# A Mamba2 scan that feeds a four-branch feed-forward merge: the spreads of two chunks, the weight sums' places and the last step's order are changed

## The chip, the cores and the metric

The kernel runs on one core of one Trainium2 chip. The time is the device time of one execution in microseconds (us); the profile is of one such execution. Engines: TensorE (PE, its weight loads PEld), VectorE (DVE), ScalarE (ACT), GpSimd (POOL) and SyncE (SP), which here only issues DMAs. PSUM banks hold 512 fp32 per partition.

## What is computed

All is fp32. First a state-space attention per batch (4), head (8) and 768 positions, with head size 32 and state size 16; `la = log(clip(a))`:

```python
L = exp(cum[i] - cum[j]) * causal          # decays inside a chunk
y = (C @ B.T * L) @ x + (C @ state) * exp(cum)
state = exp(sum(la)) * state + sum_j(B_j x_j * exp(cum[-1] - cum_j))
```

Its output, 3072 tokens of 256 channels, is the input of four feed-forward branches (256 to 1024 to 256), merged by normalised probabilities `p`:

```python
h = maximum(x @ w1[e], 0)
out += p[:, e:e+1] * (h @ w2[e])
```

The kernel works with chunks of 128 positions, since the result doesn't depend on the chunk length.

## The kernel before

**Tiling.** There are 24 chunks of 128 tokens; four of them, one from each batch, make a block of 512 tokens, and six blocks make the run. For each block the feed-forward part takes 8 steps (four branches, two halves of the hidden size), 48 in all, numbered n; r is the step's number in its block.

**Attention of a chunk** (chunks 0 to 3 stand ahead of the loop, L694 to L770). `spread` multiplies the chunk's decays by ones, so that each partition has all of them in PSUM; a_q holds them on one partition in 32, and four row tiles of 32 partitions (L322) do four quarters of 256 columns each. `decays` runs VectorE scans over them (L355) and gives the lower triangle LT; GpSimd multiplies its last column with B (L360). `masks` (ScalarE, L369) prepares C from the chunk's tokens `xb`, `scores` multiplies it with B (L384) into four quarters g, `masked` (VectorE, L396) multiplies g by LT. For chunks 0 and 1 one quarter goes `aside`: ScalarE copies it (L403) and GpSimd multiplies (L404). `outputs` multiplies by the tokens (L430), and ScalarE copies the result to yT and A (L439 to L446). From chunk 3 on the decays come spread from DRAM (`load_decays`, L125), where `store_decays` has put them.

**The gate.** `turn_gates` transposes the probabilities (L288), ScalarE copies them (p_sb, L291), SyncE stores them (L292), `spread_gate` (L300) spreads those of block 0. The bank of that spread comes from a ring of two (tag "att") that the y of the chunks use as well.

**Feed-forward by seven products.** Each pair of 2x2 block products is done with seven products in place of eight (from step 2 on): `fmul` (L491) the first ones, with `snap` (ScalarE), `total`, `gated` and `diff` (VectorE) between, and `smul` (L576) the second ones, one step later. They need four sums of weight blocks. In the first block `sum_w1` and `sum_w2` make them on GpSimd, four adds and one store each (L180 to L198); later blocks load them. GpSimd works in program order, and a step's sums wait for nothing but their weights.

**The order is written out by hand.** Every engine takes its instructions in program order; the loop L774 to L868 writes one step. A step's VectorE order is: total 11, gated 11, then the work left from the step before (two `diff`, L520, and a `carry` of a state, L454 to L461), the first half of a chunk's scan if the step has one (r of 0, 2, 4, 5), `total` 22 (L503), which TensorE's next products into bank Y (L491) wait for, and so on.

**The end.** `finish` does the last step's second products in the order 1, 3, 6, 7, 5, 2, 4, adds them to the four quarters of o (channels by tokens; d is the half of the channels, b1 and b2 the halves of the tokens), turns each back by TensorE (L627), copies it to SBUF and stores whole rows: one store of 256 KB and two of 128 KB. Blocks ahead of the last are turned by VectorE in blocks of 32 (`turned_out`, L665) and leave by `leave`: eight stores of 16 KB for each chunk, in pieces of 32 numbers, on SyncE's queue (L673).

Of the kernel before, what the change touches and what calls it, by code (L numbers as in the profile page):

```python
# [12 lines left out]
P = 128  # L13
# [4 lines left out]
def kernel(  # L18
# [255 lines left out]
    nc.gpsimd.tensor_copy(a_cut, a_sb)  # L274
    nc.gpsimd.memset(a_cut[:, :, 0:1], 0.0)

    def store_decays(kind):
        d, sb = ((acut_d, a_cut), (ac_d, a_sb))[kind]
        nc.scalar.dma_start(
            out=d.rearrange("c h s -> (c h) s").rearrange("(p r) s -> p r s", r=2), in_=sb)  # L280

    gate = {}

# [27 lines left out]

    yT, yS = {}, {}

    def spread(c, homes):


        s = st[c]
        s["a"] = []
        for q, (pool, tag) in enumerate(homes):
            k = slice(32 * q, 32 * q + 32)  # L320
            b = pool.tile([P, NT * P], FP32, tag=tag, name="a")
            nc.tensor.matmul(  # L322
                out=b, lhsT=ones[k], rhs=a_q[k, c].rearrange("p t s -> p (t s)"),
                start=True, stop=True, tile_position=(32 * q, 0))
            s["a"].append(b)

    def decays(c):
        for part in range(3):
            decay_part(c, part)
# [60 lines left out]
    def masked(cs, rs):  # L390
        for r in rs:
            for c in cs:
# [1 line left out]
                h = slice(NT * q, NT * q + NT)  # L394
                s = st[c]
                nc.vector.tensor_mul(s["MT"][:, h, 0:P], s["g"][q], s["LT"][:, h])  # L396

    def aside(c, q):

        s = st[c]  # L400
        h = slice(NT * q, NT * q + NT)
        g = att.tile([P, NT, P], FP32, tag="gs", name="gs")
        nc.scalar.copy(out=g, in_=s["g"][q])  # L403
        nc.gpsimd.tensor_mul(s["MT"][:, h, 0:P], g, s["LT"][:, h])  # L404

    state = {}

# [201 lines left out]
    def finish(n):  # L609


        k = n // SPB
        add = nc.vector.tensor_add
        b1, b2 = slice(0, HB), slice(HB, BLK)
        o = ffn.tile([P, 2, BLK], FP32, tag="o", name="o", bufs=1)
        u = ffn.tile([P, 3, HB], FP32, tag="u", name="u", bufs=1)
        turned, rows = {}, {}

        def turn_out(b, d):
            if b not in turned:  # L620
                rows[b] = ffn.tile([P, 2, DM], FP32, tag="z", name="rows", bufs=3)
                turned[b] = [ps_f.tile([P, DM], FP32, tag=tag, name="turned") for tag in "XY"] \
                    if b == 0 else ps_att.tile([P, 2, DM], FP32, tag="att", name="turned")
            for i in range(2):
                lo = b * HB + i * P
                t = turned[b][i] if b == 0 else turned[b][:, i]
                nc.tensor.transpose(t[:, d * P:d * P + P], o[:, d, lo:lo + P], ident[:, 0])  # L627

        def dst(b):
            return out.rearrange("(i k p) m -> k p i m", k=NBLK, p=P)[k][:, 2 * b:2 * b + 2]  # L630

        smul(n, 1)
        smul(n, 3)
        keep(k, 0)
        p1, p3 = kept[k, 0][:, 0], kept[k, 0][:, 1]
        smul(n, 6)
        add(u[:, 0], acc[k, 2][:, 0], p1)
        add(u[:, 1], u[:, 0], p3)
        smul(n, 7)
        smul(n, 5)  # L640
        p7, p5 = acc[k, 1][:, 0], acc[k, 1][:, 1]
        add(u[:, 2], p7, u[:, 0])
        add(o[:, 1, b2], p5, u[:, 2])
        add(o[:, 0, b2], p5, u[:, 1])
        smul(n, 2)
        add(o[:, 0, b1], acc[k, 2][:, 1], p1)
        turn_out(1, 1)
        smul(n, 4)
        turn_out(1, 0)
        nc.scalar.copy(out=rows[1], in_=turned[1])  # L650
        nc.sync.dma_start(out=dst(1), in_=rows[1])
        turn_out(0, 0)
        add(o[:, 1, b1], acc[k, 3][:, 0], u[:, 2])
        turn_out(0, 1)
        nc.vector.tensor_copy(rows[0][:, 0], turned[0][0])
        nc.sync.dma_start(out=dst(0)[:, 0], in_=rows[0][:, 0])
        nc.scalar.copy(out=rows[0][:, 1], in_=turned[0][1])
        nc.scalar.dma_start(out=dst(0)[:, 1], in_=rows[0][:, 1])

    def turned_out(k):  # L660

# [2 lines left out]
        ot = kept[k, "ot"] = ffn.tile([P, 2, BLK // 32, 32], FP32, tag="ot", name="ot", bufs=1)  # L664
        nc.vector.transpose(ot.rearrange("p d b j -> p d (b j)"), o)  # L665

    def leave(k, c):

        dst = out.rearrange(
            "(c k b i) (d a j) -> c k a d i b j", k=NBLK, i=32, b=P // 32, j=32, d=2)[c, k]  # L670
        for q in range(P // 32):
            for d in range(2):
                nc.sync.dma_start(  # L673
                    out=dst[q, d],
                    in_=kept[k, "ot"][32 * q:32 * q + 32, d, P // 32 * c:P // 32 * (c + 1)])

    def opened(n):

# [3 lines left out]


    homes = ((ps_s, "acc0"), (ps_s, "acc1"), (ps_att, "att"), (ps_att, "att"))
    banks = ((ps_f, "X"), (ps_f, "Y"), (ps_s, "acc2"), (ps_s, "acc3"))

    def turn(n, w=4):

# [4 lines left out]

    turn(1)  # L694
    turn(1, 2)
    spread(0, banks)
    turn(1, 3)
    masks(0)
    scores([0], homes)
    decays(0)  # L700
    masks(1)
    spread(1, banks)
    aside(0, 3)
    masked([0], (2, 0, 1))
    store_decays(0)
    turn_gates(ps_att, "att")
    store_decays(1)
    outputs([0])
    scores([1], ((ps_s, "acc0"), (ps_s, "acc1"), (ps_att, "att"), (ps_f, "X")))
    decays(1)  # L710
    aside(1, 3)
    spread_gate(ps_att, "att")
    masked([1], (0, 1, 2))
    spread(2, ((ps_s, "acc2"), (ps_s, "acc3"), (ps_f, "Y"), (ps_s, "acc0")))
    masks(2)
    outputs([1])
    sum_w1(0, 0)
    load_decays(3)
    load_w2(1)
# [54 lines left out]
    for n in range(PLAIN, NS):  # L774
        k, r = divmod(n, SPB)

        ahead = CPB * (k + 1)
        scanned = [ahead + d for d in {0: [0], 2: [1], 4: [2], 5: [3]}.get(r, [])]
        scored = [ahead + d for d in {3: [0, 1], 6: [2, 3]}.get(r, [])]
        done = [ahead + d for d in {4: [0, 1], 7: [2, 3]}.get(r, [])]  # L780
        if k == NBLK - 1:
            scanned, scored, done = [], [], []
        ending = r == 0 and k > 0
        e = r // JJ
        if r % JJ == 0 and n + JJ < NS:
            load_gate(*divmod(n // JJ + 1, E))
        if PLAIN + 2 < n + 2 < NS:
            load_w1(n + 2)
            load_w2(n + 2)
        opened(n)  # L790
        total(n, 1, "11")
        gated(n, "11", "z11")
        for work in late:
            work()
        if r == 1 and k > 0:
            combine(k - 1, 0)
            combine(k - 1, 1)
        for c in scanned:
            decay_part(c, 0)
        for c in scored:  # L800
            masks(c)
        if k > 0 and 2 <= r < CPB + 2:
            leave(k - 1, r - 2)
        smul(n - 1, 1)
        fmul(n, 6)
        snap(n, 6)
        smul(n - 1, 3)
        if ending:
            keep(k - 1, 0)
        if done:  # L810
            outputs(done)
            states.extend(done)
        fmul(n, 5)
        fmul(n, 7)
        snap(n, 7)
        total(n, 7, "22")
        smul(n - 1, 7)
        smul(n - 1, 5)
        if ending:
            keep(k - 1, 1)  # L820
        gated(n, "22", "z22")
        if r == 1 and k > 0:
            combine(k - 1, 2)
        for c in scanned:
            decay_part(c, 1)
        for c in scored:
            decay_part(c, 2)
        if n == PLAIN:
            sum_w2(0, 1)
        elif n == SPB - 4:  # L830
            sum_w1(n + 2)
        elif n >= SPB - 3:
            sum_w2(n)
        if n < CPB:
            load_chunk(n + CPB)
        for c in scanned if n >= CPB else []:
            if c + 2 < NCH:
                load_decays(c + 2)
        for c in done:
            if c + CPB < NCH:  # L840
                load_tokens(c + CPB)
                load_heads(c + CPB)
        fmul(n, 3)
        total(n, 6, "12")
        fmul(n, 4)
        gated(n, "21", "X")
        gated(n, "12", "z12")
        if r == SPB - 1 and k < NBLK - 1:
            sums(k + 1)
        smul(n - 1, 6)  # L850
        if scored:
            scores(scored, ((ps_att, "att"), (ps_att, "att"), (ps_f, "Y"), (ps_f, "X")))
            masked(scored, (3, 2, 0, 1))
        smul(n - 1, 2)
        diff(n, "T3", "22", "12")
        smul(n - 1, 4)
        if n == PLAIN:
            sum_w2(1, 1)
        if n != SPB - 4:
            sum_w1(n + 2)  # L860
        if PLAIN < n < SPB - 4:
            sum_w2(n + 1)
        diff(n, "T1", "12", "11")
        if r == 1 and k > 0:
            turned_out(k - 1)
        late = [lambda n=n: diff(n, "T2", "22", "T1"), lambda n=n: diff(n, "T4", "21", "T2")]
        if states:
            late.append(lambda c=states.pop(0): carry(c))  # L868
# [48 lines left out]
```

## Time and profile before

| | |
|---|---|
| median of 3 runs | 639.71 us (639.64 to 640.04) |
| profiled execution | 639.64 us, of which the span is 637.9 |
| busy: TensorE, VectorE, ScalarE, GpSimd | 632.2, 483.7, 119.1, 109.7 us |
| first feed-forward product (L540) starts | 13.29 us |
| steps 5 and 6 of the loop | 78.02 to 90.10, 90.10 to 103.87 us |
| last block's first product in `finish` | 626.40 us |
| last store issued, last byte moved | 634.55, 636.5 us |

A line of the timeline gives the start, the time, the engine (a q behind its name: its queue, for DMAs and waits), the line of the code, the operation, out<-in by the program's names, the shape, and how many instructions were merged into the line (consecutive ones of the same kind; each fp32 product counts as two). In square brackets is the idle time ahead of it and what ended it. A line of the waits gives the waiter, what it waited for, and the total, the number and the longest in us. For a DMA the time is that of its issue; the transfer comes later.

### The profile page before, as it was taken

The page shows a single profiled execution, that of the slowest core. Times are in us where ns is not written, and L with a number is a line of the kernel's source. Part 1 is how long each engine was busy: PE and PEld are TensorE (multiplying, and loading weights), DVE is VectorE, ACT ScalarE, POOL GpSimd, SP SyncE. Part 2 cuts the span into 40 slices and gives each one's busy share as a digit, 9 for nine tenths or more (in the row PEclk, how much of TensorE's full clock was granted, in tenths as well). Part 3 has the DMA queues.
Part 4 walks back from the last instruction along what each step waited for, and adds up shares of the span by engine and source line. Part 5 has one row for each costly group of instructions (what it writes and reads, how often), then busy time and mean ns, then how long its engine had stood idle before and what let it go on. Part 6 is the DMA issues. An engine that isn't in the chain of part 4 may idle for free.

```text
span 637.9 us, 9231 instructions
## 1 busy us (share of the span) xinstructions
PE 632.2 (99%) x3407; PEld 537.1 (84%) x3407; DVE 483.7 (76%) x811; ACT 119.1 (19%) x259; POOL 109.7 (17%) x159
## 2 busy tenths in 40 slices
PE   9999999999999999999999999999999999999997
PEld 5888887888888888888888888888888888888886
DVE  7869998887787688777687778768877667756555
ACT  4011221212111221122211211212121211111110
POOL 6788556020000002000002000001100000100000
PEclk9999999999999999999999999999999999999999
DMA  7987893855766392666284567639364834266000
GB/s 231 320 317 271 288 340 136 288 178 167 189 200 237 94 364 73 230 190 242 92 293 142 172 202 189 230 121 341 97 207 152 275 136 133 63 181 210 1 1 33
DMA packets 97248, 121.61 MB, mean 191 GB/s; under 512 B 28840, under 2 KB 80436, under 8 KB 97204
## 3 DMA queue, kind: packets, MB, share of 16 engines
q1 hardware_dynamic: 94376, 111.20, 53.6%
q0 software_dynamic: 2304, 9.44, 3.8%
q8 instruction: 27, 0.44, 0.3%
q10 hardware_dynamic: 524, 0.39, 0.2%
q14 instruction: 17, 0.14, 0.1%
HBM read 108.16 MB, written 12.83 MB: 190 GB/s over the span
## 4 chain that ended last, share of the span: by engine, by line
PE 98%; DVE 1%; ACT 0%; issue 0%; DVEq 0%
PE acc L576 43%; PE X L491 25%; PE Y L491 19%; PE acc L557 2%; PE y L430 2%; PE g L384 2%; PE X L540 1%; PE Y L540 1%; PE y L418 1%; PE t L691 1%; PE a L322 0%; DVE hT L520 0%; DVE h L513 0%; DVE z L503 0%; PE gp L300 0%; PE turned L627 0%
## 5 line engine op out<-in xcount | busy, mean ns | idle before, releaser
L503 DVE TENSOR_TENSOR z<-Y,snap 128x512 f32<-128x512 f32 x138 | 94.6, 685 | 123.5 <-ACT snap L498 72.7
L576 PE MATMUL acc<-hT,wt 128*128 128x256 f32 x736 | 181.2, 379 | 0.0
L498 ACT COPY snap<-X 128x512 f32<-128x512 f32 x138 | 80.8, 586 | 464.6 <-PE X L491 388.1
L576 PEld LDWEIGHTS acc<-hT,wt 128*128 128x128 f32 x736 | 139.8, 190 | 19.0
L576 PE MATMUL acc<-h,wt 128*128 128x256 f32 x552 | 142.5, 381 | 0.0
L491 PE MATMUL X<-yS,wt 128*128 128x256 f32 x552 | 141.7, 379 | 0.0
L576 PEld LDWEIGHTS acc<-h,wt 128*128 128x128 f32 x552 | 104.1, 190 | 17.1 <-issue 3.0
L491 PEld LDWEIGHTS X<-yS,wt 128*128 128x128 f32 x552 | 104.8, 190 | 14.5 <-issue 0.3
L513 DVE SCALAR_TENSOR_TENSOR h<-z,gate 128x512 f32<-128x512 f32 x138 | 100.1, 726 | 3.5 <-PE acc L557 0.4
L491 PE MATMUL Y<-yT,wt 128*128 128x256 f32 x368 | 94.7, 380 | 0.1
L491 PEld LDWEIGHTS Y<-yT,wt 128*128 128x128 f32 x368 | 68.7, 190 | 11.3 <-DVE z L503 0.8
L520 DVE TENSOR_TENSOR hT<-h,hT 128x512 f32<-128x512 f32 x92 | 65.2, 708 | 1.8
L520 DVE TENSOR_TENSOR hT<-h,h 128x512 f32<-128x512 f32 x92 | 65.7, 755 | 1.1
L355 DVE TENSOR_TENSOR_SCAN LT<-ab,ident 128x512 f32<-128x512 f32 x42 | 52.1, 1242 | 0.0
L491 PE MATMUL Y<-yS,wt 128*128 128x256 f32 x184 | 48.3, 385 | 0.0
L491 PE MATMUL X<-yT,wt 128*128 128x256 f32 x184 | 47.2, 379 | 0.0
L360 POOL TENSOR_TENSOR MT<-xb,LT 128x128 f32<-128x128 f32 x20 | 8.5, 427 | 207.5 <-DVE LT L355 102.0
L491 PEld LDWEIGHTS Y<-yS,wt 128*128 128x128 f32 x184 | 34.1, 190 | 6.4 <-issue 1.1
L491 PEld LDWEIGHTS X<-yT,wt 128*128 128x128 f32 x184 | 35.0, 190 | 4.8
L513 DVE SCALAR_TENSOR_TENSOR h<-X,gate 128x512 f32<-128x512 f32 x50 | 34.3, 685 | 6.2 <-PE X L491 3.4
L396 DVE TENSOR_TENSOR MT<-g,LT 128x256 f32<-128x256 f32 x94 | 32.4, 416 | 5.8 <-PE g L384 5.8
L341 POOL TENSOR_TENSOR cts<-ctm,dec 128x256 f32<-128x256 f32 x20 | 14.1, 724 | 129.1 <-DVE dec L338 129.1
(96 smaller groups left out, 320.9 us busy)
## 6 DMA issues: line engine op xcount, KB each, us to landing
wt<-in_w_dram SPq DMA_DIRECT2D x112, 256.0 KB
wt<-w_d SPq DMA_DIRECT2D x40, 640.0 KB
wt<-w_d SPq DMA_DIRECT2D x40, 512.0 KB
ab<-acut_d SPq DMA_DIRECT2D x21, 512.0 KB
gate<-p_d SPq DMA_DIRECT2D x23, 256.0 KB
w_d<-wt POOLq DMA_DIRECT2D x8, 640.0 KB, 4.0
wt<-in_w_dram SPq DMA_DIRECT2D x40, 128.0 KB
xb<-in_xbc_dram SPq DMA_DIRECT2D x14, 320.0 KB
```

Of the source, the lines that this page charges most:

```text
L341: nc.gpsimd.tensor_mul(cts, s["ctm"], dec.unsqueeze(1).to_broadcast([HN, NT, P]))
L355: nc.vector.tensor_tensor_scan(out=LT[:, i * w:i * w + w], data0=s["a"][i], data1=ident.rearrange("p h s -> p (h s)")[:, :w], initial=0.0, ...
L384: nc.tensor.matmul(out=g.rearrange("p t s -> p (t s)"), lhsT=s["xb"][k, OBT:OBT + P], rhs=s["ctm"][k].rearrange("p t s -> p (t s)"), start ...
L396: nc.vector.tensor_mul(s["MT"][:, h, 0:P], s["g"][q], s["LT"][:, h])
L430: nc.tensor.matmul(out=y[32 * q:32 * q + 32, t, 0:w], lhsT=s["xb"][:, h * D:h * D + D], rhs=s["MT"][:, NT * q + t, 0:w], start=(k == 0 and ...
L491: nc.tensor.matmul(out=f[bank][:, j], lhsT=wt1[n][:, w, j * P:j * P + P], rhs=rhs, start=(i in (1, 2, 5) and j == 0), stop=(j == JJ - 1), ...
L498: nc.scalar.copy(out=s, in_=first[n]["X"])
L503: nc.vector.tensor_add(z, first[n]["Y"], first[n][i])
L513: nc.vector.scalar_tensor_tensor(out=h, in0=first[n][src], scalar=0.0, in1=g.unsqueeze(1).to_broadcast([P, JJ, HB]), op0=ALU.max, op1=ALU. ...
L520: nc.vector.tensor_sub(h[o], h[x], h[y])
L540: nc.tensor.matmul(out=f[bank][:, j], lhsT=wt1[n][:, w, j * P:j * P + P], rhs=yT[k][:, i, cols], start=(i == 0 and j == 0), stop=(i == 1), ...
L576: nc.tensor.matmul(out=acc[k, u][:, half], lhsT=w2_op(n, w)[:, j], rhs=rhs[:, j], start=(begins and j == 0), stop=(n % SPB == SPB - 1 and ...
```

## The change

- **Spreads.** The spread of chunk 0 is as before. Those of chunks 1 and 2 are done by products over all 128 partitions, whose weights are a mask of 32 rows; two quarters share a bank (X, then Y), so that a scan takes 512 columns. The two halves of chunk 2's spread are placed apart, the second behind the outputs of chunk 1.
- **Order ahead of the loop.** `aside` is gone: VectorE does all four quarters. The two decay stores stand together, `masks(2)` stands ahead of the outputs of chunk 0, and `turn_gates` behind the scores of chunk 1.
- **Weight sums.** `sum_w2(5)` moves from the middle of step 5 to the end of step 4, `sum_w2(7)` from the middle of step 7 to the end of step 6.
- **The last step.** The order is 1, 2, 6, 7, 4, 5, 3. The two quarters of the first half of the tokens are turned by VectorE in blocks of 32 and leave by eight 16 KB stores each, the first on SyncE and GpSimd in turn, the second on SyncE (five) and ScalarE (three). The other two quarters are turned by TensorE; one leaves by a store of 128 KB, the last by two of 64 KB.

```diff
--- before.py
+++ after.py
@@ -274,10 +274,11 @@
     nc.gpsimd.tensor_copy(a_cut, a_sb)
     nc.gpsimd.memset(a_cut[:, :, 0:1], 0.0)
 
-    def store_decays(kind):
-        d, sb = ((acut_d, a_cut), (ac_d, a_sb))[kind]
+    def store_decays():
         nc.scalar.dma_start(
-            out=d.rearrange("c h s -> (c h) s").rearrange("(p r) s -> p r s", r=2), in_=sb)
+            out=acut_d.rearrange("c h s -> (c h) s").rearrange("(p r) s -> p r s", r=2), in_=a_cut)
+        nc.scalar.dma_start(
+            out=ac_d.rearrange("c h s -> (c h) s").rearrange("(p r) s -> p r s", r=2), in_=a_sb)
 
     gate = {}
 
@@ -311,18 +312,28 @@
 
     yT, yS = {}, {}
 
-    def spread(c, homes):
+    def spread(c, halves=(0, 1)):
 
 
         s = st[c]
-        s["a"] = []
-        for q, (pool, tag) in enumerate(homes):
-            k = slice(32 * q, 32 * q + 32)
-            b = pool.tile([P, NT * P], FP32, tag=tag, name="a")
-            nc.tensor.matmul(
-                out=b, lhsT=ones[k], rhs=a_q[k, c].rearrange("p t s -> p (t s)"),
-                start=True, stop=True, tile_position=(32 * q, 0))
-            s["a"].append(b)
+        if c == 0:
+            s["a"] = []
+            for q, (pool, tag) in enumerate(((ps_f, "X"), (ps_f, "Y"), (ps_s, "acc2"), (ps_s, "acc3"))):
+                k = slice(32 * q, 32 * q + 32)
+                b = pool.tile([P, NT * P], FP32, tag=tag, name="a")
+                nc.tensor.matmul(
+                    out=b, lhsT=ones[k], rhs=a_q[k, c].rearrange("p t s -> p (t s)"),
+                    start=True, stop=True, tile_position=(32 * q, 0))
+                s["a"].append(b)
+            return
+        for i in halves:
+            b = ps_f.tile([P, 2, NT * P], FP32, tag="XY"[i], name="a")
+            for q in range(2):
+                nc.tensor.matmul(
+                    out=b[:, q], lhsT=qmask[:, 2 * i + q, 0:1].to_broadcast([P, P]),
+                    rhs=a_q[:, c].rearrange("p t s -> p (t s)"), start=(q == 0), stop=True,
+                    skip_group_check=True)
+            s.setdefault("a", []).append(b.rearrange("p q s -> p (q s)"))
 
     def decays(c):
         for part in range(3):
@@ -394,14 +405,6 @@
                 h = slice(NT * q, NT * q + NT)
                 s = st[c]
                 nc.vector.tensor_mul(s["MT"][:, h, 0:P], s["g"][q], s["LT"][:, h])
-
-    def aside(c, q):
-
-        s = st[c]
-        h = slice(NT * q, NT * q + NT)
-        g = att.tile([P, NT, P], FP32, tag="gs", name="gs")
-        nc.scalar.copy(out=g, in_=s["g"][q])
-        nc.gpsimd.tensor_mul(s["MT"][:, h, 0:P], g, s["LT"][:, h])
 
     state = {}
 
@@ -614,48 +617,53 @@
         b1, b2 = slice(0, HB), slice(HB, BLK)
         o = ffn.tile([P, 2, BLK], FP32, tag="o", name="o", bufs=1)
         u = ffn.tile([P, 3, HB], FP32, tag="u", name="u", bufs=1)
-        turned, rows = {}, {}
-
-        def turn_out(b, d):
-            if b not in turned:
-                rows[b] = ffn.tile([P, 2, DM], FP32, tag="z", name="rows", bufs=3)
-                turned[b] = [ps_f.tile([P, DM], FP32, tag=tag, name="turned") for tag in "XY"] \
-                    if b == 0 else ps_att.tile([P, 2, DM], FP32, tag="att", name="turned")
-            for i in range(2):
-                lo = b * HB + i * P
-                t = turned[b][i] if b == 0 else turned[b][:, i]
-                nc.tensor.transpose(t[:, d * P:d * P + P], o[:, d, lo:lo + P], ident[:, 0])
-
-        def dst(b):
-            return out.rearrange("(i k p) m -> k p i m", k=NBLK, p=P)[k][:, 2 * b:2 * b + 2]
-
+        p1 = ffn.tile([P, 2, HB], FP32, tag="kept0", name="kept0", bufs=1)[:, 0]
+        ot = kept[k, "ot"] = ffn.tile([P, 2, BLK // 32, 32], FP32, tag="ot", name="ot", bufs=1)
+
+        def leave_first(d, queues):
+
+            w = HB // 32
+            nc.vector.transpose(ot[:, d, :w].rearrange("p b j -> p (b j)"), o[:, d, b1])
+            for i, queue in enumerate(queues):
+                c, q = divmod(i, P // 32)
+                leave_part(k, c, q, d, queue)
+
+        def turn(d, i, pool, tag):
+            t = pool.tile([P, P], FP32, tag=tag, name="turned")
+            lo = HB + i * P
+            nc.tensor.transpose(t, o[:, d, lo:lo + P], ident[:, 0])
+            return t
+
+        dst = out.rearrange("(i k p) (d m) -> k d p i m", k=NBLK, p=P, d=2)[k][:, :, 2:4]
+        rows = ffn.tile([P, 2, 2, P], FP32, tag="z", name="rows", bufs=3)
         smul(n, 1)
-        smul(n, 3)
-        keep(k, 0)
-        p1, p3 = kept[k, 0][:, 0], kept[k, 0][:, 1]
+        nc.scalar.copy(out=p1, in_=acc[k, 0][:, 0])
+        smul(n, 2)
+        add(o[:, 0, b1], acc[k, 2][:, 1], p1)
+        leave_first(0, [nc.sync, nc.gpsimd] * 4)
         smul(n, 6)
         add(u[:, 0], acc[k, 2][:, 0], p1)
-        add(u[:, 1], u[:, 0], p3)
         smul(n, 7)
+        add(u[:, 1], acc[k, 1][:, 0], u[:, 0])
+        smul(n, 4)
+        add(o[:, 1, b1], acc[k, 3][:, 0], u[:, 1])
+        leave_first(1, [nc.sync, nc.scalar] * 3 + [nc.sync] * 2)
         smul(n, 5)
-        p7, p5 = acc[k, 1][:, 0], acc[k, 1][:, 1]
-        add(u[:, 2], p7, u[:, 0])
-        add(o[:, 1, b2], p5, u[:, 2])
-        add(o[:, 0, b2], p5, u[:, 1])
-        smul(n, 2)
-        add(o[:, 0, b1], acc[k, 2][:, 1], p1)
-        turn_out(1, 1)
-        smul(n, 4)
-        turn_out(1, 0)
-        nc.scalar.copy(out=rows[1], in_=turned[1])
-        nc.sync.dma_start(out=dst(1), in_=rows[1])
-        turn_out(0, 0)
-        add(o[:, 1, b1], acc[k, 3][:, 0], u[:, 2])
-        turn_out(0, 1)
-        nc.vector.tensor_copy(rows[0][:, 0], turned[0][0])
-        nc.sync.dma_start(out=dst(0)[:, 0], in_=rows[0][:, 0])
-        nc.scalar.copy(out=rows[0][:, 1], in_=turned[0][1])
-        nc.scalar.dma_start(out=dst(0)[:, 1], in_=rows[0][:, 1])
+        add(o[:, 1, b2], acc[k, 1][:, 1], u[:, 1])
+        add(u[:, 2], acc[k, 1][:, 1], u[:, 0])
+        smul(n, 3)
+        turned = ps_f.tile([P, 2, P], FP32, tag="X", name="turned")
+        for i in range(2):
+            lo = HB + i * P
+            nc.tensor.transpose(turned[:, i], o[:, 1, lo:lo + P], ident[:, 0])
+        add(o[:, 0, b2], acc[k, 0][:, 1], u[:, 2])
+        nc.scalar.copy(out=rows[:, 1], in_=turned)
+        nc.sync.dma_start(out=dst[1], in_=rows[:, 1])
+        for i, (pool, tag, copy, queue) in enumerate((
+                (ps_f, "Y", nc.vector.tensor_copy, nc.sync), (ps_att, "att", nc.scalar.copy, nc.scalar))):
+            t = turn(0, i, pool, tag)
+            copy(out=rows[:, 0, i], in_=t)
+            queue.dma_start(out=dst[0][:, i], in_=rows[:, 0, i])
 
     def turned_out(k):
 
@@ -664,15 +672,18 @@
         ot = kept[k, "ot"] = ffn.tile([P, 2, BLK // 32, 32], FP32, tag="ot", name="ot", bufs=1)
         nc.vector.transpose(ot.rearrange("p d b j -> p d (b j)"), o)
 
-    def leave(k, c):
-
+    def leave_part(k, c, q, d, queue):
         dst = out.rearrange(
             "(c k b i) (d a j) -> c k a d i b j", k=NBLK, i=32, b=P // 32, j=32, d=2)[c, k]
+        queue.dma_start(
+            out=dst[q, d],
+            in_=kept[k, "ot"][32 * q:32 * q + 32, d, P // 32 * c:P // 32 * (c + 1)])
+
+    def leave(k, c):
+
         for q in range(P // 32):
             for d in range(2):
-                nc.sync.dma_start(
-                    out=dst[q, d],
-                    in_=kept[k, "ot"][32 * q:32 * q + 32, d, P // 32 * c:P // 32 * (c + 1)])
+                leave_part(k, c, q, d, nc.sync)
 
     def opened(n):
 
@@ -682,7 +693,7 @@
 
 
     homes = ((ps_s, "acc0"), (ps_s, "acc1"), (ps_att, "att"), (ps_att, "att"))
-    banks = ((ps_f, "X"), (ps_f, "Y"), (ps_s, "acc2"), (ps_s, "acc3"))
+    banks = ((ps_s, "acc2"), (ps_s, "acc3"), (ps_s, "acc0"), (ps_s, "acc1"))
 
     def turn(n, w=4):
 
@@ -693,27 +704,25 @@
 
     turn(1)
     turn(1, 2)
-    spread(0, banks)
+    spread(0)
     turn(1, 3)
     masks(0)
     scores([0], homes)
     decays(0)
     masks(1)
-    spread(1, banks)
-    aside(0, 3)
-    masked([0], (2, 0, 1))
-    store_decays(0)
+    spread(1)
+    store_decays()
+    masks(2)
+    masked([0], range(NQ))
+    outputs([0])
+    scores([1], banks)
+    decays(1)
     turn_gates(ps_att, "att")
-    store_decays(1)
-    outputs([0])
-    scores([1], ((ps_s, "acc0"), (ps_s, "acc1"), (ps_att, "att"), (ps_f, "X")))
-    decays(1)
-    aside(1, 3)
+    spread(2, (0,))
     spread_gate(ps_att, "att")
-    masked([1], (0, 1, 2))
-    spread(2, ((ps_s, "acc2"), (ps_s, "acc3"), (ps_f, "Y"), (ps_s, "acc0")))
-    masks(2)
+    masked([1], range(NQ))
     outputs([1])
+    spread(2, (1,))
     sum_w1(0, 0)
     load_decays(3)
     load_w2(1)
@@ -829,7 +838,7 @@
             sum_w2(0, 1)
         elif n == SPB - 4:
             sum_w1(n + 2)
-        elif n >= SPB - 3:
+        elif n == SPB - 2:
             sum_w2(n)
         if n < CPB:
             load_chunk(n + CPB)
@@ -858,7 +867,7 @@
             sum_w2(1, 1)
         if n != SPB - 4:
             sum_w1(n + 2)
-        if PLAIN < n < SPB - 4:
+        if PLAIN < n != SPB - 3:
             sum_w2(n + 1)
         diff(n, "T1", "12", "11")
         if r == 1 and k > 0:
```

## The prediction

> **What bounds the kernel now.** I read the chain that ended last first, then the waits of TensorE, then the timeline at the three places that the diff touches: the head (to 15 us), loop steps 5 and 6 (78.02 to 103.87 us), and the end.
>
> ```profile
> PE 98%; DVE 1%; ACT 0%; issue 0%; DVEq 0%
> ...
> PE X L540 <- ACT yT L439: 0.5, 1, 0.5
> ```
>
> TensorE is the chain. Its own waits hold, beyond the first instruction, one entry: the first FFN products (X, L540) wait 0.46 us for ScalarE's copy of yT. From there on TensorE is busy in nearly every slice, so whatever moves that start, or opens a gap later, moves the end by as much. The head, from the timeline:
>
> ```profile
> 8.50 2.42 DVE L355 TENSOR_TENSOR_SCAN LT<-a,ident 128x256 f32<-128x256 f32 x4
> ...
> 10.84 1.06 DVE L396 TENSOR_TENSOR MT<-g,LT 128x256 f32<-128x256 f32 x3
> ...
> 10.16 1.16 PE L300 MATMUL gp<-p_sb,ident 96*128 96x128 f32 x8
> 11.25 0.74 PE L322 MATMUL a<-a_q,ones 32*128 32x256 f32 x8
> 12.04 0.78 PE L430 MATMUL y<-MT,xb 128*32 128x144 f32 x16
> 13.29 1.99 PE L540 MATMUL X<-yT,wt 128*128 128x256 f32 x8 [0.46 <-ACT yT L439]
> ...
> SPq L292 <- DMA xb<-in_xbc_dram: 1.9, 1, 1.9
> ```
>
> The reader should see that VectorE's scans and masks of chunk 1 end at 11.9, that y of chunk 1 follows at 12.04, and that SyncE's queue, free at 8.49, waited 1.9 us for a load of xb: the tokens of chunk 2 landed at about 10.4. Then the stretch in which GpSimd's sums of weights meet VectorE:
>
> ```profile
> 80.11 0.59 POOL L192 DMA_DIRECT2D w_d<-wt  x1 [0.30 <-POOL wt L184]
> 87.42 0.40 POOL L360 TENSOR_TENSOR MT<-xb,LT 128x128 f32<-128x128 f32 x1 [6.71 <-DVE LT L355]
> 92.83 0.73 POOL L180 TENSOR_TENSOR wt<-wt 128x256 f32<-128x256 f32 x1
> ...
> 80.58 0.69 DVE L513 SCALAR_TENSOR_TENSOR h<-z,gate 128x512 f32<-128x512 f32 x1
> 81.18 1.41 DVE L520 TENSOR_TENSOR hT<-h,hT 128x512 f32<-128x512 f32 x2
> 83.25 1.22 DVE L355 TENSOR_TENSOR_SCAN LT<-ab,ident 128x512 f32<-128x512 f32 x1
> 84.71 0.69 DVE L503 TENSOR_TENSOR z<-Y,snap 128x512 f32<-128x512 f32 x1 [0.25 <-ACT snap L498]
> 92.66 1.46 DVE L513 SCALAR_TENSOR_TENSOR h<-z,gate 128x512 f32<-128x512 f32 x1
> 94.05 2.34 DVE L520 TENSOR_TENSOR hT<-h,hT 128x512 f32<-128x512 f32 x2
> 97.27 0.69 DVE L503 TENSOR_TENSOR z<-Y,snap 128x512 f32<-128x512 f32 x1
> ```
>
> In step 6 GpSimd adds beside VectorE, and h and the two hT take 1.46 and 2.34 us; in step 5 GpSimd is idle from 80.70 to 87.42 and the same instructions take 0.69 and 1.41. The second z of step 6 ends at 97.96, and TensorE's Y, due at 97.71, starts at 98.01. Last, the end and the price of a small store:
>
> ```profile
> 634.52 0.41 SPq L656 DMA_DIRECT2D out_dram<-rows  x1
> 634.55 0.36 ACTq L658 DMA_DIRECT2D out_dram<-rows  x1
> ...
> 143.68 3.67 SPq L673 DMA_DIRECT2D out_dram<-ot  x8
> 571.19 7.89 SPq L673 DMA_DIRECT2D out_dram<-ot  x8
> ```
>
> **Head.** Removed: two ScalarE copies and two GpSimd products (aside, 0.36 and 0.73 us each), nobody's bound. Added: the fourth masked product of chunks 0 and 1 on VectorE. Three advance it by 8.50-7.52 = 0.98, so one costs 0.33. Four scans of 256 advance it by 2.34, two of 512 (chunk 3, 18.50 to 20.74) by 2.24; from PSUM I take 2.3. VectorE then runs scan 1 from 8.83, masks 1 from 11.13, done at about 12.45. The spreads of chunks 1 and 2 become four full products: two are x4 instructions, 0.86 in the steady chain, against 0.65 for all four row tiles. Spread 1 is covered by TensorE's wait for masks 0 (8.9); uncovered it would cost 1.1.
>
> The step that I price highest is masks(2), which ScalarE now does ahead of its copies of y0. It waits for chunk 2's tokens. Early bound of their landing: all loads up to them are 1.67 MB, and the moved bytes reach 1.73 MB at 9.0; chunk 1's tokens needed 0.82 MB, reached at 6.05, and released ScalarE at 7.10, so add 1.0: about 10.0. The wait line gives 10.4, which I take. Behind it on ScalarE: the masks (0.69, to 11.1), yT and A of chunk 0 (9.62 to 10.08 now, 0.46), p_sb (0.26, to 11.8). The gate's spread needs p_sb and the bank that those copies free: 11.9, for 1.08; y1 13.0, for 0.64; then the second half of spread 2, which is put behind y1, 0.86. X starts at 14.5 and not 13.29: **+1.2**. If the tokens are there in time, TensorE's queue (g1 to 10.2, pp 0.25, half a spread 0.9, gate 1.1, y1 held by the last mask, half a spread) gives 14.0: +0.75; a landing 0.3 later than the wait line would make +1.5. SyncE's p_d store moves from 10.47 to about 11.9; the decay load behind it waits for acut_d until 13.3 either way. The two decay stores leave ScalarE at 7.9 and 8.3, ahead of masks(2). Scan 2's second half ends near 16.0; y2 uses it at 19.0.
>
> **Weight sums.** w2's sums for step 5 move from 87.80 to directly behind w1's of step 6, where GpSimd's queue is free at 80.70; nothing it reads is late (loaded by SyncE from 54.39). The sums that stood at 92.83 take its place at 87.80. So step 5 gets what step 6 had: there the sums start 0.17 us after h, here 0.12 after. From h to behind the carry, step 6 takes 97.27-92.66 = 4.61 us, step 5 83.25-80.58 = 2.67: 1.94 more. Step 5 has a scan (1.13) behind it that step 6 has not. Its z moves from 84.71 to 80.58+4.61+1.13 = 86.32, ends at 87.01, and Y, due at 85.62, starts at 87.06: +1.44. In step 6 the 0.30 is given back: **+1.14**. Bounds: nothing lost, -0.30 (step 4's stretch, where GpSimd ends at 68.9, takes only 2.43 from h); above, +1.7, as a scan beside GpSimd at 40.93 took 1.74 and not 1.22. The sums of step 7 move in the program only: GpSimd goes from 104.19 straight to them at 104.81 now. The earlier store crosses loads at 80 to 92; TensorE waits for no weights there, and if that cover went, a 512 KB load at 344 GB/s would be 1.5.
>
> The Trainium skill (SBUF — State Buffer, Who interferes with whom) calls the port pair of VectorE and GpSimd an exclusive lock: an instruction with two SBUF inputs may be held for a whole GpSimd instruction. By that rule the five such instructions up to the scan could each lose one of 0.73, an estimate of 3.65 in place of the row's 1.94, and the sum would be 1.7 higher; the row stays.
>
> **End.** Now seven products and four transposes stand before the last result: TensorE's last product starts at 632.13 and ends at 633.0. Afterwards seven products from 626.40, 0.864 each, end at 632.45, the fifth at 630.71. Operands: T2 and T4 are ready at 628.2, before need. Added on VectorE: two 32-block turns of 128x256, by the rows 128x32 (0.20) and 128x1024 (1.24) 0.44 each. First quarter: add 628.33, turned 629.2; second: add 630.92, turned 631.8. Each goes out in eight stores of 16 KB. SyncE's price per store: 0.458 with quiet queues (3.67 for 8), 0.74 to 0.99 beside weight loads (7.89 for 8). No loads run in the last 10 us, so 0.458: four stores from 629.25, done 631.1; five from 631.85, done 634.14; then the third quarter's store to 634.6 and the last result's from 634.6. What is queued behind: ScalarE's copy of the turned block waits behind three stores (631.85 to 633.2), is done at 633.6, and SyncE is later. GpSimd's four at about 0.9 (0.59 and the 0.30 ahead of it) start their last at 632.0; its 640 KB stores land in 4.0, of which 1.9 is data at 344 GB/s, so 16 KB by 634.1, and at the full 4.0 by 636.0, when the last result lands too.
> The last issue is thus where it was (634.55), but behind it stand few bytes. Now 512 KB run from 634.95 to 636.5 at 344 GB/s; then 0.94 from issue to first byte, 64 KB at 0.19: 635.73. The 1.4 us from last byte to the end of the span stay: **-0.77**. Bounds: -1.0; with pieces at half the rate, -0.3; with stores at 0.75, +1.1; at 0.99, +3.2.
> The Trainium skill (DMA: Bandwidth & Descriptors, Specifications) wants at least 512 B per piece for full rate and speaks of read-modify-write below; the two early quarters leave in pieces of 128 B, so this rule speaks against the change. The row is the quiet group of eight: a DMA share of 0.16 at 26 GB/s, limited by its issues. [...]
>
> **Sum.** The profiled execution took 639.64, 0.07 under the median of the runs, 639.71: 1.74 around a span of 637.9. 639.64 + 1.2 + 1.14 - 0.77 = 641.2.
>
> **Rivals.**
> *VectorE holds its time in step 5* (not slower). The cover is 0.25 us of idle before z and 0.17 behind it; GpSimd loses as well when the two meet, and may lose all. Then 639.64 + 1.2 - 0.30 - 0.77 = 639.8. It decides at a stall of 1.2 us: below that the sum is within 0.2%. Against it stands step 6, the same instructions at the same offset.
> *SyncE's queue bounds the end.* At 0.75 per store the last result leaves at 636.5 and the sum is 643.1; the end loses from 0.61 per store on. For it, most groups of the trace; against it, the idle queues.
> *Chunk 2's tokens are there in time.* Head +0.75, sum 640.7. For it the byte count; against it the wait line.
>
> **How the numbers follow.** Forecast 0.48, own range 640.5 to 642.0; step 5 holds 0.17; SyncE's queue 0.15; tokens in time 0.14; head and end both far better 0.06. A measurement tells 0.2%, 1.28 us, from no change: the border lies at 641.0. Slower: 0.39 of the forecast, 0.15, 0.04 = 0.58; same: 0.09, 0.14, 0.10 = 0.33; faster: 0.03 and 0.06 = 0.09. The range 639.3 to 643.2 leaves out the upper half of the queue case and the far better one.
>
> **What would show it.** ScalarE waiting for xb near 10 us and X starting at 14.5; GpSimd's sums at 81.4 to 86 (the head's delay added) with h near 1.4, and Y of step 5 about 1.4 late; no gap in step 6; SyncE's stores 0.46 apart at the end, last bytes 0.8 earlier beside the last product. The prediction is wrong if z of step 5 ends before TensorE asks, or if stores take 0.7.

## The result and the profile after

The changed kernel takes 642.55 us (median of 4 runs, 642.12 to 642.7) where the kernel before takes 639.75 on the same chip (median of 4): a ratio of 1.0042, 95% interval 1.0025 to 1.0059. It is 2.8 us slower; 1.5 was forecast. The profiled execution has a span of 640.8 us, 2.9 more than before. Its first lines to read are TensorE's own waits: waiter, what it waited for, then total, count and longest in us.

```profile
PE Y L494 <- DVE z L506: 1.2, 1, 1.2
PE gp L301 <- ACT p_sb L292: 1.1, 1, 1.1
PE t L702 <- DVE ones L206: 1.1, 1, 1.1
PE acc L579 <- DVE o L642: 0.6, 1, 0.6
PE g L395 <- ACT ctm L380: 0.3, 1, 0.3
PE turned L634 <- DVE o L659: 0.3, 1, 0.3
```

Before, the only one past the first instruction was the 0.5 for yT. Three new ones matter: the gate's spread waits for p_sb (head), Y waits for z (step 5), and a product of the last step (acc) waits for VectorE's o (end). The timeline of the head (start, time, engine, line, operation; in brackets the idle time ahead and what ended it):

```profile
10.85 0.69 ACT L380 ACTIVATE ctm<-xb,tmask 128x128 f32<-128x128 f32 x2 [2.71 <-DMA xb<-in_xbc_dram]
11.45 0.35 ACT L442 COPY yT<-y 128x256 f32<-128x256 f32 x1
11.78 0.26 ACT L292 COPY p_sb<-pp 96x128 f32<-96x128 f32 x1
...
12.10 1.16 PE L301 MATMUL gp<-p_sb,ident 96*128 96x128 f32 x8 [1.06 <-ACT p_sb L292]
13.18 0.70 PE L433 MATMUL y<-MT,xb 128*32 128x144 f32 x16
13.81 1.13 PE L332 MATMUL a<-a_q,qmask 128*128 128x256 f32 x4
14.78 1.89 PE L543 MATMUL X<-yT,wt 128*128 128x256 f32 x8
```

ScalarE stands 2.71 us for chunk 2's tokens, y0's copies and p_sb follow it, TensorE waits 1.06 for p_sb, and X starts at 14.78 in place of 13.29. TensorE's first product of step 5 starts at 79.29, 1.44 later than before (77.85). In step 5, from the same view:

```profile
82.17 0.74 POOL L180 TENSOR_TENSOR wt<-wt 128x256 f32<-128x256 f32 x1
...
82.01 1.46 DVE L516 SCALAR_TENSOR_TENSOR h<-z,gate 128x512 f32<-128x512 f32 x1
83.39 2.34 DVE L523 TENSOR_TENSOR hT<-h,hT 128x512 f32<-128x512 f32 x2
86.61 1.22 DVE L366 TENSOR_TENSOR_SCAN LT<-ab,ident 128x512 f32<-128x512 f32 x1
87.75 0.67 DVE L506 TENSOR_TENSOR z<-Y,snap 128x512 f32<-128x512 f32 x1
...
88.47 1.13 PE L494 MATMUL Y<-yT,wt 128*128 128x256 f32 x4 [1.25 <-DVE z L506]
```

GpSimd's sums start 0.16 us behind h; h and the two hT take the 1.46 and 2.34 that step 6 had, and Y starts 2.85 later than before (85.62): 1.44 of the head and 1.41 of its own. Step 6 has no gap any more, so the first product of step 7 starts at 106.25, 2.55 later (103.70). Up to the last block's first product in `finish` this stays so: 628.94 against 626.40. The end:

```profile
628.94 1.89 PE L579 MATMUL acc<-h,wt 128*128 128x256 f32 x8
...
630.94 0.42 DVE L642 TENSOR_TENSOR o<-acc,kept 128x256 f32<-128x256 f32 x1 [0.18 <-PE acc L579]
...
631.42 3.72 PE L579 MATMUL acc<-hT,wt 128*128 128x256 f32 x16 [0.59 <-DVE o L642]
631.87 5.59 SPq L678 DMA_DIRECT2D out_dram<-ot  x9
...
637.55 0.40 SPq L661 DMA_DIRECT2D out_dram<-rows  x1
638.05 0.44 SPq L666 DMA_DIRECT2D out_dram<-rows  x1
```

The four instructions of product 6 were due at 630.67 (628.94 and two products of 0.865) and start at 631.42, right behind VectorE's add, which reads the other half of their bank: 0.75 late. SyncE's last store is issued 9.11 us behind the first product; before it was 8.15 (634.55 less 626.40). From there to the end of the span it is 2.75, before 3.35. So the last step costs 0.96 and gives back 0.60: +0.36. With 2.54 ahead of it, that is the 2.9 of the spans. SyncE's queue has a share in it: the last block of results was copied to SBUF at 637.17, but its store stood behind the others on that queue until 638.05.

### The profile page after: what moved, and what is told of

It is laid out like the page before. It is cut to its first block, busy times and chain, and to the rows that moved or that the text cites. A ratio compares the mean times of both kernels' runs of the same rounds, so it can differ in the third digit from the quotient of the medians.

```text
span 640.8 us, 9243 instructions
## 1 busy us (share of the span) xinstructions
PE 632.4 (99%) x3403; PEld 537.7 (84%) x3403; DVE 484.9 (76%) x811; ACT 118.0 (18%) x257; POOL 110.8 (17%) x161
## 4 chain that ended last, share of the span: by engine, by line
PE 96%; DVE 1%; DMA 1%; SPq 0%; ACT 0%; issue 0%; ACTq 0%; POOL 0%; DVEq 0%; POOLq 0%
PE acc L579 43%; PE X L494 25%; PE Y L494 19%; PE acc L560 2%; PE y L433 2%; PE g L395 2%; PE X L543 1%; PE Y L543 1%; DMA xb<-in_xbc_dram 1%; PE y L421 1%; DVE hT L523 0%; DVE h L516 0%; DVE z L506 0%; DVE LT L366 0%; SPq L152 0%
```

## Experiments

Where a run is compared with the kernel before, it was measured beside it on the same chip (639.98 with the first four, 640.01 with the next four, 639.95 with the last). Times are medians of 10 or 11 runs, 7 for the bank run; intervals are of the ratio to the kernel before.

### One part of the change at a time

**Weight sums alone**, in the kernel before:

```diff
-        elif n >= SPB - 3:
+        elif n == SPB - 2:
             sum_w2(n)
...
-        if PLAIN < n < SPB - 4:
+        if PLAIN < n != SPB - 3:
             sum_w2(n + 1)
```

> The kernel before with only the weight sums moved as in the change. Theory (GpSimd's adds of step 5 beside VectorE make the z of step 5 late, and step 6 is relieved): Y of step 5 starts about 1.4 us late, at 87.0 in place of 85.62, the gap ahead of Y in step 6 (0.30) is gone, and the time is 1.1 us over the kernel before (640.9). Rival (the gap in the changed kernel needs the later head as well, or a late transfer): no gap in step 5, time as before within 0.3 us.

Measured: 641.07, ratio 1.0018 (1.0010 to 1.0027), +1.1 us. TensorE's waits and products, from its timeline:

```profile
83.91 1.89 PE L576 MATMUL acc<-hT,wt 128*128 128x256 f32 x8
87.04 1.13 PE L491 MATMUL Y<-yT,wt 128*128 128x256 f32 x4 [1.24 <-DVE z L503]
...
97.50 1.89 PE L576 MATMUL acc<-hT,wt 128*128 128x256 f32 x8
99.23 1.03 PE L491 MATMUL Y<-yT,wt 128*128 128x256 f32 x4
```

Y of step 5 starts at 87.04, where the working had 87.06, and Y of step 6 follows without a gap. The head and the end play no part in it.

**The part ahead of the loop alone**, the rest as before:

```diff
-    spread(1, banks)
-    aside(0, 3)
-    masked([0], (2, 0, 1))
-    store_decays(0)
+    spread(1)
+    store_decays()
+    masks(2)
+    masked([0], range(NQ))
...
-    spread(2, ((ps_s, "acc2"), (ps_s, "acc3"), (ps_f, "Y"), (ps_s, "acc0")))
-    masks(2)
     outputs([1])
+    spread(2, (1,))
```

> The kernel before with only the part ahead of the loop changed (spreads, four masked quarters on VectorE, order of masks, stores and gate). Theory: X of the first feed-forward products starts at 14.6 to 14.8 us in place of 13.29, all later work is shifted by that, step 6 keeps its gap of 0.30: 1.4 us over the kernel before (641.2). Rival (later waits for DMA absorb the shift): under 0.7 us over.

Measured: 640.68, ratio 1.0016 (1.0007 to 1.0024), +0.7 by the medians, with runs from 640.47 to 642.31. The profiled execution is a late one (641.93):

```profile
11.75 0.69 ACT L380 ACTIVATE ctm<-xb,tmask 128x128 f32<-128x128 f32 x2 [3.73 <-POOL MT L371]
...
13.00 1.16 PE L301 MATMUL gp<-p_sb,ident 96*128 96x128 f32 x8 [1.43 <-ACT p_sb L292]
...
15.68 1.89 PE L543 MATMUL X<-yT,wt 128*128 128x256 f32 x8
```

The masks of chunk 2 start at 11.75, and X follows at 15.68. (The release is put down to GpSimd's product, which came last; that product has nothing to do with the tokens.) So the head's term isn't one number: it depends on when the tokens land in that execution, and its middle is below the 1.4 that I expected here. In this execution the load was also issued later, at 5.34 in place of 4.74, behind a load that took 1.03 to issue. Step 6 keeps its gap: its product ahead of Y starts at 98.27 and takes 1.73, Y starts at 100.30.

**The last step alone** (`finish` and `leave_part` as in the change, the rest as before):

> The kernel before with only the last step changed. Theory (the gain from fewer last bytes is eaten by TensorE's wait for VectorE's read of the other half of a bank): product 6 waits about 0.75 us for the first quarter's add, and the time is 0.3 to 0.4 us over the kernel before (640.1). Rival (the end in the changed kernel was late for another reason, such as the shifts ahead of it): 0.8 us under the kernel before, as predicted.

Measured: 640.15, ratio 1.0004 (0.9995 to 1.0012). By the time this can't be told from no change, nor from +0.3. The trace can:

```profile
629.41 3.72 PE L576 MATMUL acc<-hT,wt 128*128 128x256 f32 x16 [0.59 <-DVE o L639]
...
636.05 0.44 SPq L663 DMA_DIRECT2D out_dram<-rows  x1
```

It has the same wait of 0.59 for VectorE's o, SyncE's last store 9.12 us behind the first product (636.05 less 626.93), 2.75 from there to the end. The gain of 0.77 that was forecast isn't there, whatever stands ahead of it.

By their medians the three parts alone add 1.1, 0.7 and 0.2, 2.0 together, where the whole change adds 2.6 to 2.8. No run here says where the rest comes from; the head's share moves from execution to execution.

### The wait in the last step

The changed kernel with two products exchanged:

```diff
-        smul(n, 6)
-        add(u[:, 0], acc[k, 2][:, 0], p1)
         smul(n, 7)
+        smul(n, 6)
+        add(u[:, 0], acc[k, 2][:, 0], p1)
         add(u[:, 1], acc[k, 1][:, 0], u[:, 0])
```

> The changed kernel with product 7 ahead of product 6 in the last step, so that the product behind the first quarter's add writes another bank than the one being read. Theory (the wait is for the bank): no wait of TensorE ahead of the sixth or seventh product, the second quarter's stores still start about 0.75 us earlier, and the time is 0.7 us under the changed kernel (641.8). Rival (the wait is for the operand T2 or T3 of the late differences): the wait moves to product 7 and the time stays at 642.5.

Measured: 641.51, ratio 1.0038 (1.0022 to 1.0055). The interval overlaps that of the changed kernel, so the time doesn't settle it. The trace does, in TensorE's waits and then in the timeline:

```profile
PE Y L494 <- DVE z L506: 1.2, 1, 1.2
...
PE turned L634 <- DVE o L659: 0.3, 1, 0.3
...
PE gp L301 <- ACT p_sb L292: 0.2, 1, 0.2
```

```profile
630.06 4.00 PE L579 MATMUL acc<-hT,wt 128*128 128x256 f32 x16
630.34 0.42 DVE L642 TENSOR_TENSOR o<-acc,kept 128x256 f32<-128x256 f32 x1 [0.18 <-PE acc L579]
...
632.93 0.73 PEld L579 LDWEIGHTS acc<-hT,wt 128*128 128x128 f32 x4 [0.51 <-DVE u L647]
...
636.72 0.43 SPq L666 DMA_DIRECT2D out_dram<-rows  x1
```

The wait of a product for o is gone: product 7 starts at 630.06, ahead of VectorE's add, and the operands were there. So the rival, an operand that comes late, is out. Whether the program waits for the buffer or for the bank can't be told apart, since each of these buffers is one whole bank. The last store is issued 8.38 us behind the first product (628.34) in place of 9.11. The sixteen instructions now take 4.00 and not 3.72: product 5, whose weights wait 0.51 for VectorE's u, is held by the read of product 7 from the same bank, a smaller case of the same thing.

### ScalarE's queue in the head

The changed kernel with the masks of chunk 2 later:

```diff
     store_decays()
-    masks(2)
     masked([0], range(NQ))
...
     masked([1], range(NQ))
+    masks(2)
     outputs([1])
```

> The changed kernel with the masks of chunk 2 put behind the masked quarters of chunk 1, after all of ScalarE's copies that the gate needs. Theory (ScalarE's queue stood behind the late tokens): no wait of TensorE for p_sb, X of the first feed-forward products starts at 13.9 to 14.1 whenever the tokens land, 0.3 to 1.5 us under the changed kernel, and its times scatter less. Rival (the second half of chunk 2's spread and the fourth mask set the start): X stays where it is in the changed kernel.

The changed kernel itself, measured beside it:

> The changed kernel once more, beside the next ones. Theory (three separate terms, the head's set by when chunk 2's tokens land): 2.2 to 2.9 us over the kernel before; ScalarE's masks of chunk 2 start when the tokens land (10.2 to 11.8 us so far) and X follows 3.9 us behind.

Measured: with the masks later 642.06 (641.63 to 643.83), ratio 1.0030 (1.0018 to 1.0043); the changed kernel 642.59 (641.91 to 645.13), ratio 1.0041 (1.0026 to 1.0056). The intervals overlap; 0.5 between the medians. In this pair both profiled executions have X at 14.2: the tokens were early in the changed one. Put together, the executions give a pattern:

| execution | ScalarE starts masks of chunk 2 | X starts | difference |
|---|---|---|---|
| changed kernel, second time | 10.01 | 14.21 | 4.20 |
| bank run | 10.29 | 14.21 | 3.92 |
| zeros run (below) | 10.61 | 14.53 | 3.92 |
| changed kernel | 10.85 | 14.78 | 3.93 |
| part ahead of the loop alone | 11.75 | 15.68 | 3.93 |
| masks later | not in the way | 14.20 | |

From 10.3 on X follows the start of the masks at 3.92 to 3.93. In the bank and the zeros run the trace puts the masks' release down to TensorE; in all five executions, though, SyncE's own wait for this load ended about 0.1 ahead of the masks. The kernel before doesn't depend on that load: in the run of the last step alone, which has its head, SyncE waited for the load until about 11.5, and X started at 13.49.

With the tokens at 10.01, and with the masks out of the way, X starts at 14.2 and no earlier. There TensorE has no wait from 8 to 16 us: y0, scores, pp, half a spread, the gate, y1 and half a spread stand one behind the other. That is the half of the rival for this run that names the spread; the fourth mask plays no part, since the last mask of chunk 1 ends at 12.46, ahead of y1 (12.61). But 14.2 isn't a fixed floor. In both of these executions TensorE was late from the start: the product t (ones by ones) ahead of the scores took 1.65, in the changed kernel's first profile 0.91, and y0 began at 9.3 in place of 8.5. As the tokens were early in both, no run shows the later masks with late tokens; that ScalarE's wait makes up the rest is read from the table, not tested.

The kernel before isn't free of scatter either: in profiled executions of kernels with its head X started at 13.29, 13.30, 13.49, 13.63 and 14.10, the last two with that product at 1.65. Against 13.29 a start at 14.2 costs 0.9, against these two 0.6 and 0.1. What moves it there was not tried.

### What in the sums holds VectorE

The changed kernel without the four adds for step 5; GpSimd fills blocks with zeros in their place:

```diff
+        if n == SPB - 3:
+            for w in (S1, S2, S4, S1, S2, S4):
+                for _ in range(2):
+                    nc.gpsimd.memset(w2_op(n, w), 0.0)
+            nc.gpsimd.dma_start(out=w2_d[n], in_=wt2[n][:, 2 * HB:])
-        if n < SPB:
+        elif n < SPB:
             sums_of(lambda w: w2_op(n, w), part)
```

> The changed kernel in which the four adds of w2's sums for step 5 are left out, so that these sums are wrong; in their place GpSimd fills three of the blocks with zeros, twelve times, and then stores as before. GpSimd is busy for about as long (some 3.7 us after 80.7 us and the head's delay), but reads nothing. Theory (VectorE's instructions with two operands in SBUF lose to GpSimd's reads): h stays at 0.69 and the two hT at 1.41, Y of step 5 starts without a gap, and the time is 1.4 us under the changed kernel (641.2). Rival (any GpSimd work, or the store behind it, holds VectorE or the products): h and hT as long as in the changed kernel, and the gap of 1.4 us stays.

Measured: 641.08, ratio 1.0022 (1.0011 to 1.0034), 1.1 over the kernel before, where the changed one is 2.6 to 2.8 over it.

```profile
81.89 3.81 POOL L198 MEMSET wt<- 128x256 f32 x12
85.99 0.53 POOL L199 DMA_DIRECT2D w_d<-wt  x1 [0.30 <-POOL wt L198]
...
81.75 0.69 DVE L521 SCALAR_TENSOR_TENSOR h<-z,gate 128x512 f32<-128x512 f32 x1
82.36 1.41 DVE L528 TENSOR_TENSOR hT<-h,hT 128x512 f32<-128x512 f32 x2
...
85.07 1.89 PE L584 MATMUL acc<-hT,wt 128*128 128x256 f32 x8
86.80 1.03 PE L499 MATMUL Y<-yT,wt 128*128 128x256 f32 x4
```

GpSimd is busy for 3.81 us at the same place and stores as before, and VectorE runs at its undisturbed 0.69 and 1.41; Y has no gap. So neither GpSimd's being busy nor the store holds VectorE; the adds do. That it is their reads is not shown by this run alone, as an add differs from a fill in more than that (0.74 to 1.17 us each in the changed kernel, the fills 0.32). This agrees with the Trainium skill (SBUF — State Buffer, Who interferes with whom): an instruction of VectorE with two inputs in SBUF contends with one of GpSimd that reads SBUF, not with one that only writes it.

### A version that beats both

From the kernel before, with the changed kernel's last step, edited to take up what the runs showed (the main lines, against that last step). The order is 1, 2, 7, 6, 4, 5, 3:

```diff
+        smul(n, 7)
+        p7 = ffn.tile([P, 2, HB], FP32, tag="kept1", name="kept1", bufs=1)[:, 0]
+        nc.scalar.copy(out=p7, in_=acc[k, 1][:, 0])
         smul(n, 6)
         add(u[:, 0], acc[k, 2][:, 0], p1)
-        smul(n, 7)
-        add(u[:, 1], acc[k, 1][:, 0], u[:, 0])
+        add(u[:, 1], p7, u[:, 0])
...
-        leave_first(1, [nc.sync, nc.scalar] * 3 + [nc.sync] * 2)
         smul(n, 5)
+        sooner = ps_f.tile([P, 2, P], FP32, tag="Y", name="sooner")
+        for i in range(2):
+            nc.tensor.transpose(sooner[:, i], o[:, 1, i * P:i * P + P], ident[:, 0])
+        nc.scalar.copy(out=early, in_=sooner)
+        nc.sync.dma_start(out=whole[1][:, 0:2], in_=early)
```

> The kernel before with a new last step: the change's order with product 7 ahead of 6, product 7 copied out by ScalarE so that product 5 needn't wait for VectorE's read, only the first quarter by 16 KB stores, the second turned by TensorE and stored by one store of 128 KB. Theory (TensorE's waits for a bank and SyncE's queue were what ate the gain): no wait of TensorE between the seven products, the last store is issued 0.8 us earlier against the last product than in the changed kernel, 0.8 to 1.0 us under the kernel before (639.0). Rival (the last transfers bound the end whatever is ahead of them): as before within 0.3.

Measured: 639.18 (638.54 to 639.62), ratio 0.9982 (0.9969 to 0.9994), 0.8 us under the kernel before.

```profile
628.82 3.62 PE L576 MATMUL acc<-hT,wt 128*128 128x256 f32 x16
630.02 1.74 SPq L683 DMA_DIRECT2D out_dram<-ot  x4
...
634.24 0.40 SPq L666 DMA_DIRECT2D out_dram<-rows  x1
634.79 0.36 SPq L671 DMA_DIRECT2D out_dram<-rows  x1
634.87 0.36 ACTq L671 DMA_DIRECT2D out_dram<-rows  x1
```

None of the seven products waits (sixteen instructions in 3.62), and the last store is issued 7.78 us behind the first product (627.09): 0.37 earlier than in the kernel before, 1.33 earlier than in the changed one. SyncE's last store no longer stands in its queue: its block is copied at 634.76 and the store issued at 634.79. From the last store to the end it is 2.83, 0.52 less than before. Several things were changed at once here, so the gain can't be divided among them.

With w1's sums of step 7 moved from the end of step 5 to the middle of step 6:

> The same with the weight sums w1 of step 7 put to the middle of step 6, behind the products of C and the decays. Theory (these sums beside VectorE made the gap of 0.30 in step 6): Y of step 6 starts without a gap and the time is 0.3 us under the one before it in this list. Rival: the sums, now later, hold VectorE in step 7, or step 7's products wait for them: no gain or a loss.

Measured: 639.66, ratio 0.9991 (0.9978 to 1.0003): no gain. The gap of step 6 is gone, as expected, and a new one stands in step 7, the second half of the rival:

```profile
98.52 1.03 PE L491 MATMUL Y<-yT,wt 128*128 128x256 f32 x4
...
106.70 1.03 PE L491 MATMUL X<-yS,wt 128*128 128x256 f32 x4
108.22 1.13 PE L576 MATMUL acc<-h,wt 128*128 128x256 f32 x4 [0.50 <-POOL wt L182]
```

TensorE waits for w2's sums of step 6, now behind those of w1: due at 107.57, started at 108.22.

## Why the prediction was right or wrong

**Direction and range:** slower, as forecast; 642.55 lies in the range but over the likeliest case's own (640.5 to 642.0). The sum missed 1.35 us: 0.25 in the head, 1.1 at the end, nothing in the middle. That the range held is partly luck: its part above 642.0 was there for a SyncE queue at 0.75 us per store, which didn't happen, and was filled by a wait that the sum had at nothing.

**Head, +1.2: right in mechanism, sized by one number that varies.** ScalarE did stand for chunk 2's tokens, and the steps behind it took together about what their rows said: 3.93 from the masks' start to X, where the working had 4.1. The tokens came at 10.85 and not 10.4, which the profile of the kernel before couldn't tell better; other executions had 10.0 to 11.75. In the profile the term is 1.44, against the earliest of the five starts seen with the old head. The case "tokens in time" happened too (10.01), at +0.9 and not +0.75: there spread 1, which the working had covered by the masks, ended behind them (9.4), and scores of chunk 1 ended at 10.6 where the working had 10.2. The price of the fourth mask, 0.33, could be read (four took the next scan from 7.16 to 8.46, 0.325 each); two scans of 512 from PSUM took 2.25, a bit under my 2.3.

**Weight sums, +1.14: right within 0.03.** +1.41 and -0.30 make 1.11 in the profile, 1.1 alone. The step that carried it was to take step 6's own rows as the price of the same instructions at the same offset from GpSimd's sums, and to add the one scan that step 6 hasn't. "VectorE holds its time" is refuted, and the zeros run shows what it would have taken.

**End, -0.77: wrong.** The step that failed is "seven products from 626.40, 0.864 each, end at 632.45": it took TensorE to run through and checked only whether operands were ready. Product 6 writes one half of bank acc2 while VectorE reads the other half, and the program waits for that read: 0.75. The kernel before has no such pair in its last step, so no row showed it. The Trainium skill asks for such a wait (PSUM — Partial Sum Buffer, PSUM bank collisions raise a hardware error): accesses of two engines are to be kept apart by bank, not by address. I had not asked for it in the working. The wait of 0.59 and its end with the add are this case's row for it, and the bank run removes both. The other 0.38: SyncE's last store was issued 0.16 later than the working has behind that wait (638.05 against 637.89), and 2.75 and not 2.53 passed from there to the end. What made these two longer was not tried.

**SyncE's price per store: right.** The five of the second quarter took 2.21, 0.44 each, against 0.458; the rival with 0.75 is refuted. From the same trace, from 635 us on:

```profile
635.24 2.21 SPq L678 DMA_DIRECT2D out_dram<-ot  x5
```

But "behind it stand few bytes" hid something that my own row had: the quiet group of eight moved 26 GB/s at a DMA share of 0.16, which would be about 163 GB/s at full share (an estimate), half the 344 of the last block's big stores. In the changed kernel the second quarter moves at 67 GB/s and a share of 0.42 from 636.0 to 637.5, 160 at full share. So by this estimate the pieces of 128 B do cost about twice their bytes; the rule of 512 B, which names no price, had the direction right, and I read the low share as no loss. They didn't bound the end: from 636.0 to 637.5 about 100 of the second quarter's 128 KB had gone, and the last two stores on SyncE came at 637.55 and 638.05.

## What to carry to other kernels

When products are put in a new order, check for each one who still reads the bank that it writes, the other half of it too, and not only whether its operands are ready. A wait put ahead of other work on an in-order queue can pass its scatter on: here the landing of one load, hidden before, set the start of TensorE's chain from 10.3 us on. Moving work on an idle engine has a price where it meets another engine's two-operand instructions; the same instructions at the same offset elsewhere in the trace give it.

## What the runs showed of the hardware that I had not expected

The landing of one 320 KB load let ScalarE start between 10.0 and 11.75 us over five executions; in the four that lie between 10.0 and 10.85 it was issued at 4.74 or 4.75, in the fifth at 5.34. GpSimd's zeros cost VectorE nothing (0.69 and 1.41), while its adds at the same place doubled h (1.46) and took the two hT to 2.34.
